# Retention attention and a top-2 mixture of experts in one kernel: k read as f32 on SyncE's queue, tails of q and k in 1-KB rows, states 64 columns wide, PSUM in pairs of banks, and a listed order in place of a planner

## The chip, the cores and the metric

The kernel runs on one core of a Trainium2 chip. Its time is the device time of one execution in microseconds (us). Three runs of the kernel before are known. Their median is 423.11 us, the lowest is 417.48 and the highest 436.01. The execution that the profiler recorded took 420.08 us.

A core has five engines with a queue of instructions each: TensorE (PE) multiplies matrices, VectorE (DVE), ScalarE (ACT) and GpSimd (POOL) work elementwise, and SyncE (SP) issues transfers (DMAs). Each queue is worked off in order: an instruction that waits holds everything behind it on its engine. Sixteen DMA engines move the data. A DMA that SyncE or ScalarE issues is shown as hardware_dynamic in the profile; GpSimd's are software_dynamic, and these alone change the type of the data on the way (f32 to bf16) or take row numbers from a table.

## The reference

```python
# q, k, v: (8 batches, 8 heads, 576 positions, 64)
scores = q @ k.T / 8
ret    = scores * where(i >= j, gamma[head] ** (i - j), 0)     # gamma[h] = 1 - 2**(-5-h)
x      = (ret @ v) as 4608 rows of 512                         # a row: one position, its 8 heads
noisy  = x @ w_gate + log1p(exp(x @ w_noise)) * noise          # 8 experts
top2   = the two largest of each row, softmax over the two as weights
out    = sum over the two: weight * (relu(x @ w1[e]) @ w2[e])  # w1: 512x1024, w2: 1024x512
```

## The kernel before

**Attention.** Work goes in 16 units. Unit u is one batch and four of its heads; four units make a pair of batches (bp 0 to 3). Only the first 512 positions of a sequence are in the units; the last 64 of each are the tail, one per pair of batches. For a unit `load` (L621) brings q, k and v, `cast` (L663) scales q and v by powers of gamma and makes them bf16, `tr` (L692) transposes k and q on TensorE, `scores` (L717) makes masked scores inside blocks of 128 positions, `states` (L751) sums k times v over blocks, and `out_` (L784) adds what the scores and the states of earlier blocks give. `tail` (L827) does the same for the last 64 positions.

How the data come: q as f32 in rows of 2 KB and v as f32 in rows of 512 bytes, both on SyncE. k comes on GpSimd (L647, `go = nc.gpsimd if n == "k"`), which turns it into bf16 on the way, so no engine casts it. The tails are three loads of two DMAs each per pair of batches (L658), all on SyncE and in rows of 256 bytes. Until the units are done, raw k lies in the buffer of expert 2's weights (class `kb`) and raw q in that of expert 1's (class `wq`), so these weights are loaded after the last unit's k and q (the argument `after` of `weights`). v lies in `big`.

A state is a 64x64 block per head, but lies in a tile of 128 columns for two heads with zeros beside it. So a state is taken out of PSUM in two halves of 64 partitions (L450 `tb<-ps`), and five tiles are set to zero first (L527). Scores and outputs leave PSUM one bank (128x512) at a time (L744, L450 `xT<-ps`).

**Routing.** When the four units and the tail of a pair of batches are done, `route` (L895) makes its logits, picks the two experts, finds each row's place in each expert's list, and writes the rows of x to the table `xd` in DRAM (L1072, on SyncE).

**Experts.** Each expert has a list of up to 1216 rows in blocks of 128. `fetch` (L1166) gathers a block from `xd` (L1179, on GpSimd) and transposes it, `up` and `wide` multiply by w1 (L1261, L1287), `relu` (L1270 on ScalarE, L1272 on VectorE) takes the result out, `second` and `halves` multiply by w2 (L1349, L1368), and `finish` (L1378) scales the rows and writes or adds them to the output (L1397 and L1399, then L1405 on GpSimd). The first blocks of experts 0 to 2 hold rows of early pairs of batches (`CLOSE`), so they can run while attention goes on: these are `up` and its `second`. The weights of experts 0 to 2 are loaded on GpSimd (L1112, L1116), the others on SyncE and cast by ScalarE or VectorE (`weights3`).

**Order.** Each call of `Plan.op` (L237) records an operation with its cost, its engine or a choice of two, and its priority. `Plan.run` (L274) goes through the recorded operations with a model of the engines and picks the one that can start first; the table `ORDER` shifts priorities by stage, and `BIAS` weighs VectorE against ScalarE where both may take it. `warm` (L454) fills expected gaps of TensorE in the first 170 us with matmuls whose result is not used (L458).

## Time and profile before

| | |
|---|---|
| runs | 423.11 us median of 3 (417.48 to 436.01) |
| profiled execution | 420.08 us, of which the span from first to last instruction is 418.5 us |
| PE busy | 378.8 us of the span (91%) |
| DVE, ACT, POOL busy | 166.6, 255.2, 302.1 us |
| mean clock granted to TensorE | 0.966 of full |
| DMA | 93.75 MB in 112584 packets, 65807 of them under 512 bytes |

The profile's page and the answers of the trace are read as follows. A row of a group of instructions has the line of the kernel, the engine, the operation, what it writes and reads (`half<-ps`: from PSUM into a tile of class half), the shapes, the count, then the busy time in us and the mean of one in ns, and then the engine's idle time just before them and what ended it. A row of a stretch (`A:B`) has its length, the busy time and count of PE, PE's weight loads (PEld), DVE, ACT and POOL, then the granted clock of TensorE, the mean busy share of the 16 DMA engines (over 1 where an engine has packets of two queues at once), and the GB/s moved, counted by the size written. A row of a source line has the shortest, middle and longest duration in ns and the first and last start in us.

### The profile page before, as it was taken

Reading aid. Unit: us, or ns where it says so; the run is one execution under the profiler, and the core shown is the slowest. Engines: PE = TensorE matmul, PEld = TensorE weight load, DVE = VectorE, ACT = ScalarE, POOL = GpSimd, SP = SyncE. Lnnn points to the kernel's source line nnn. Section 1 sums busy time; section 2 is a strip of 40 time slices with the busy share of each in tenths; the row PEclk is TensorE's granted clock in tenths of the full one; section 3 lists DMA queues with packets and bytes.
Section 4 is the critical chain, followed back from the end, with each engine's and each line's share of the span. In section 5 each row is a group of like instructions: output and inputs, shape, how many; then the busy total and the mean of one; then the engine's idle time right before and its main releaser. Section 6 shows DMA issues by size and latency. Waiting matters only on the chain. (4 is left out here: it accounts for less than half of the span.)

```text
span 418.5 us, 11275 instructions
## 1 busy us (share of the span) xinstructions
PE 378.8 (91%) x4415; PEld 235.4 (56%) x4415; DVE 166.6 (40%) x512; ACT 255.2 (61%) x432; POOL 302.1 (72%) x333
## 2 busy tenths in 40 slices
PE   5779786959989889999999999999999999999991
PEld 2457665837768667775566544544554554454461
DVE  5856578694979959220224322113112101100001
ACT  1437676746778765555567777756675676554550
POOL 8997766696399746776577767787786687753882
PEclk9999899697999969999999999999999999999997
DMA  9998999999995999579999999999999999991894
GB/s 219 266 235 189 259 228 186 296 260 257 256 231 107 257 237 254 151 177 238 243 342 383 270 259 279 239 278 223 289 236 232 183 268 182 214 152 25 130 127 105
DMA packets 112584, 93.75 MB, mean 224 GB/s; under 512 B 65807, under 2 KB 89872, under 8 KB 112530
## 3 DMA queue, kind: packets, MB, share of 16 engines
q0 software_dynamic: 34512, 40.31, 52.5%
q1 hardware_dynamic: 75330, 52.53, 49.5%
q8 instruction: 35, 0.57, 0.6%
q10 hardware_dynamic: 2688, 0.18, 0.5%
q14 instruction: 19, 0.16, 0.2%
HBM read 72.97 MB, written 26.36 MB: 237 GB/s over the span
## 5 line engine op out<-in xcount | busy, mean ns | idle before, releaser
L1349 PE MATMUL ps<-W,half 128*128 128x512 bf16 x568 | 185.1, 381 | 0.0
L1287 PE MATMUL ps<-big,W 128*128 128x512 bf16 (+4 forms) x640 | 180.6, 329 | 0.0
L1270 ACT ACTIVATE half<-ps 128x512 bf16<-128x512 f32 (+5 forms) x186 | 93.1, 506 | 77.0 <-PE ps L1287 64.0
L1179 POOL DMA_INDIRECT xg<-xd,xi x80 | 84.9, 1061 | 36.8 <-issue 15.0
L1405 POOL DMA_INDIRECT out_dram<-half,pl x59 | 79.8, 1352 | 28.4 <-ACT half L1270 13.9
L1287 PEld LDWEIGHTS <-W 128*128 128x128 bf16 x640 | 62.6, 98 | 48.7 <-issue 1.0
L1349 PEld LDWEIGHTS <-half 128*128 128x128 bf16 x568 | 55.2, 98 | 60.3 <-issue 0.6
L1212 DVE COPY pl<-xg 128x3 f32<-128x3 f32 (+1 forms) x65 | 13.4, 207 | 117.6 <-DMA xg<-xd,xi 117.5
L744 DVE TENSOR_TENSOR half<-ps,mask 128x512 bf16<-128x512 f32 x64 | 40.4, 683 | 16.0 <-PE ps L736 9.9
L450 ACT ACTIVATE half<-ps 128x1024 bf16<-128x1024 bf16 (+1 forms) x36 | 35.0, 992 | 14.5 <-PE ps L1201 6.0
L683 POOL TENSOR_TENSOR half<-big,tab 128x512 bf16<-128x512 f32 x30 | 31.9, 1080 | 7.2 <-DMA big<-in_v_dram 4.4
L450 ACT ACTIVATE W<-big 128x1024 bf16<-128x1024 f32 x34 | 35.5, 1051 | 0.0
L1261 PE MATMUL ps<-half,W 128*128 128x256 bf16 (+1 forms) x288 | 31.1, 263 | 0.1
L450 ACT ACTIVATE tb<-ps 64x512 bf16<-64x512 f32 x32 | 18.9, 592 | 18.3 <-PE ps L769 18.1
L1397 ACT ACTIVATE half<-ps,pl 128x512 f32<-128x512 f32 x42 | 28.7, 682 | 0.1
L1399 DVE TENSOR_SCALAR half<-ps,pl 64x256 f32<-64x256 f32 (+1 forms) x21 | 11.9, 570 | 39.3 <-PE ps L1368 21.3
L1405 POOL DMA_INDIRECT out_dram<-half,xg x15 | 15.4, 1026 | 16.7 <-ACT half L1397 11.5
L1261 PEld LDWEIGHTS <-W 128*128 128x128 bf16 x288 | 24.6, 101 | 4.7 <-issue 0.2
L676 POOL TENSOR_TENSOR half<-W,tabq 128x1024 bf16<-128x1024 f32 x11 | 20.9, 1903 | 5.4 <-DMA W<-in_q_dram 4.4
L450 ACT ACTIVATE xT<-ps 128x512 bf16<-128x512 f32 (+1 forms) x39 | 19.7, 555 | 6.2 <-PE ps L885 4.2
L458 PE MATMUL ps<-mask,ident__61 128*128 128x512 bf16 x67 | 18.3, 403 | 5.2 <-DVE wgn L592 5.2
L769 PE MATMUL ps<-half,W 64*64 64x64 bf16 (+2 forms) x512 | 18.8, 220 | 3.1 <-issue 2.4
(181 smaller groups left out, 425.1 us busy)
## 6 DMA issues: line engine op xcount, KB each, us to landing
big<-in_moe_w_dram SPq DMA_DIRECT2D x40, 512.0 KB
W<-in_q_dram SPq DMA_DIRECT2D x32, 256.0 KB
big<-in_v_dram SPq DMA_DIRECT2D x14, 512.0 KB
W<-in_moe_w_dram POOLq DMA_DIRECT2D x12, 512.0 KB, 13.0
xd<-xg SPq DMA_DIRECT2D x16, 264.0 KB
W<-in_k_dram POOLq DMA_DIRECT2D x14, 256.0 KB, 10.2
xg<-xd,xi POOLq DMA_INDIRECT x80, 7.2
big<-in_v_dram SPq DMA_DIRECT2D x4, 256.0 KB
```

Of the source, the lines that this page charges most:

```text
L450: self.nc.scalar.activation(out, in_, Act.Copy)
L676: self.eng(e).tensor_tensor(o, i, tabq.t[:, 2 * hq:2 * hq + 2].unsqueeze(3).to_broadcast([P, 2, 8, HD]), Alu.mult)
L683: self.eng(e).tensor_tensor(o, i, t, Alu.mult)
L744: nc.vector.tensor_tensor(S.t.bitcast(BF16).rearrange("p (h c x) -> p h c x", h=2, c=2)[:, h], p[h].t.rearrange("p (c x) -> p c x", c=2), ...
L769: nc.tensor.matmul(o[h * HD:(h + 1) * HD, hp, n, :], lhsT=self.keys(kn, hq, c, r, 2 * hp + h)[:k], rhs=vv[:k, r, c, y].unsqueeze(1).to_bro ...
L1179: ins = nc.gpsimd.indirect_dma_start(out=x.t[:n, :], out_offset=None, in_=self.xd[:rows, :], in_offset=IOff(ap=xi.t[:n, h:h + 1], axis=0), ...
L1261: nc.tensor.matmul(pv()[:, f2, :], lhsT=w.t[:, o:o + P], rhs=xv()[:, di, :n], start=(di == 0), stop=(di == KD - 1))
L1270: self.nc.scalar.activation(o, i, Act.Relu)
L1287: self.mm = nc.tensor.matmul(p.t[:, :n], lhsT=w.t[:, o:o + P], rhs=xv()[:, di, :n], start=(di == 0), stop=(di == KD - 1))
L1349: self.mm = self.nc.tensor.matmul(po.t, lhsT=hv[:, c:c + P], rhs=self.W[e].t[:, o:o + DM], start=(f == 0), stop=(f == KF - 1))
L1397: nc.scalar.activation(y.t[:n, c], x, Act.Copy, scale=g()[:n])
L1405: ins = nc.gpsimd.indirect_dma_start(out=self.out[:, :], out_offset=IOff(ap=ix()[:n], axis=0), in_=y.t[:n, :], in_offset=None, bounds_chec ...
```

## The change

- **Order.** `ORDER`, `BIAS` and the choice in `Plan.run` go. A list `PLAN` of all 1899 operations by number sets the order of recording, with `d`, `a` or `p` where an operation may go to VectorE, ScalarE or GpSimd. Slots of buffers are still chosen as the list is gone through.
- **k.** All 18 DMAs of k go on SyncE, as f32, and `cast` gets a step on ScalarE that makes k bf16 (2 halves for the first two units, one operation of 128x1024 for each other).
- **Places of raw data.** k and q of units 0 to 11 share a class `raw` in the buffers of experts 1 and 2; those of units 12 to 15 lie in `big` beside v.
- **Tails.** k and q of a tail come in rows of 1 KB: four positions of one head side by side. Each of the 16 former DMAs becomes two of 64 rows, and each of them reads 4 heads of 16 rows (`b::2`, `g`). The scale of a tail's q then depends on row and place (`tabt`, some 25 small operations ahead), its transposes are 32 of 64x64, and the copy after them puts the positions in order. v's tail is as before.
- **States.** A state tile has 64 columns per block, is taken out in one copy of 128x512, and isn't set to zero ahead; the product with it (`inter`) is made per head, 12 matmuls of 64x64 in place of 6 of 128x128, and before the scores instead of after.
- **Pairs of banks.** The two banks of scores are masked in one VectorE operation of 128x1024, and the two banks of a unit's output are copied in one. v is scaled in one operation of 128x1024 per unit (from unit 2 on) in place of two.
- **Small.** The loads of noise and gates go from ScalarE's queue to SyncE's. Some scale factors are folded into an Exp.

The listing of the orders gives these counts: ScalarE has 308 rows (429 before), VectorE 600 (464), GpSimd 317 (292), SyncE 193 (143). Of the `relu` copies 85 go to VectorE (10 before) and 111 to ScalarE (186). The matmuls of `up`, `wide`, `second`, `halves` and `column` are the same 1640; 61440 of their 638976 columns stand ahead of the last matmul of the last `route` before, and 60416 now. There are 40 unused matmuls for warming (67 before).

```diff
@@ Plan.run
-        while ready:
-            pick = None
-            for o in ready:
...
-                key = (round(t * 20), o.prio, o.i)
...
+        for x in PLAN:
+            o = self.ops[int(x.rstrip("dap"))]
+            e = {"d": "DVE", "a": "ACT", "p": "POOL"}.get(x[-1]) or list(o.eng)[0]
+            c, taken = o.eng[e], []
+            for b in o.allocs:
+                taken.append((slot(b, taken), b))
@@ Kernel.__init__
-        pl.cls("tb", mk("tb", 5, [P, 2, 4, P], BF16))
+        pl.cls("tb", mk("tb", 8, [P, 2, 4, HD], BF16))
...
-        pl.cls("kb", [(ws[2][:, i * F:(i + 1) * F], None) for i in range(8)])
-        pl.cls("wq", [(ws[1][:, 2 * i * F:2 * (i + 1) * F].bitcast(F32), None) for i in range(4)])
+        rw = [x[:, 4 * i * F:4 * (i + 1) * F].bitcast(F32).rearrange("p (c x) -> p c x", c=2) for x in ws[1:] for i in range(2)]
+        pl.cls("raw", [(x[:, i, :], x) for x in rw for i in range(2)])
@@ load
-            self.raw = {"k": [pl.buf("kb", "att") for c in range(2)], "v": [pl.buf("big", "att") for c in range(2)]}
+            self.raw = {"k": pl.buf("raw", "k", 2) if u < 12 else pl.buf("big", "k", 2), "v": pl.buf("big", "att", 2)}
...
-                go = nc.gpsimd if n == "k" else nc.sync
-                got.append(self.inp(lambda e, s=s, t=t, c=c, m=m, go=go: go.dma_start(
...
+                got.append(self.inp(lambda e, s=s, t=t, c=c, m=m: nc.sync.dma_start(
@@ load_tail
-                self.inp(lambda e, n=n, t=t, b=b: nc.sync.dma_start(
-                    out=t.t[b * HD:(b + 1) * HD].rearrange("p (h d) -> p h d", h=E),
-                    in_=self.src[n][2 * bp + b, :, 512:, :].rearrange("h s d -> s h d")),
...
+                    for c in range(2):
+                        nc.sync.dma_start(out=t.t[s, c * 256:(c + 1) * 256], in_=x[2 * bp + c, b::2, 512:, :].rearrange("h (g r) d -> h g (r d)", r=4))
@@ cast
+        def k(e, c):
+            o, i, _ = parts(rk, kn, c)
+            nc.scalar.activation(o, i, Act.Copy)
@@ scores
-            for h in range(2):
...
-                pl.op("DVE", 0.69, ev, r=[p[h], mask], w=[(S, h)], prio=u, at="scores2")
...
+            pl.op("DVE", 1.22, lambda e, p=p, S=S: nc.vector.tensor_tensor(
@@ states
-            for h in range(2):
-                s = slice(h * HD, (h + 1) * HD)
-                self.copy(e, T.t[s, :, :, s], o[s])
+            self.copy(e, T.t, p.t.rearrange("p (y n d) -> p y n d", y=2, n=4))
@@ out_
-        for e in range(2):
...
-            pl.op({"ACT": 0.6, "DVE": 0.69}, 0, ev, r=[p[e]], w=[(xT, (hq, b, e))], prio=u, at="out_3")
...
+        pl.op({"ACT": 1.03, "DVE": 1.22}, 0, ev, r=[p], w=[(xT, (hq, b, 0)), (xT, (hq, b, 1))], prio=u, at="out_3")
@@ record
-            raw = pl.fifo["kb" if e == 2 else "wq", "att"] if e else []
+            raw = pl.fifo["raw", "k"] + pl.fifo["raw", "q"] if e else []
```

Two places in the orders are shown. The first is SyncE's queue about the tail of the pair of batches 2 before; W is raw q here, big is v, half a tail, xd the table of rows.

```order
L647 DMA big_77<-in_v_dram 128x8x128 x2
L635 DMA W_123<-in_q_dram 64x2x512 x4
L647 DMA big_78<-in_v_dram 128x8x128 x2
L658 DMA half_87<-in_k_dram 64x8x64 x2
L658 DMA half_101<-in_q_dram 64x8x64
L1072 DMA xd<-xg_110 128x2x264
L658 DMA half_101<-in_q_dram 64x8x64
L1072 DMA xd<-xg_111 128x2x264
```

The same queue now, at the tail of the pair of batches 1, where W holds raw k and raw q.

```order
L514 DMA W_126<-in_k_dram 128x8x128 x2
L503 DMA W_126<-in_q_dram 64x2x512 x2
L968 DMA xd<-xg_114 128x2x264
L514 DMA big_81<-in_v_dram 128x8x128 x2
L531 DMA half_95<-in_k_dram 64x1x256 x4
L968 DMA xd<-xg_117 128x2x264
L531 DMA half_96<-in_q_dram 64x1x256 x4
L968 DMA xd<-xg_116 128x2x264
```

What moved: the units' k stands in SyncE's queue now between q and v, and a tail's k or q is four DMAs of 64 rows of 256 numbers in place of two of 512 rows of 64 numbers.

The second place is GpSimd's queue about the last units before: L647 is a DMA of k, L676 and L683 cast q and v, L841 a tail, L1179 gathers rows for an expert, L1112 and L1116 load weights into W_123 (expert 1).

```order
L647 DMA W_124<-in_k_dram 128x8x128
L841 TENSOR_TENSOR half_95<-half_97,tab 128x512
L1179 DMA xg_116<-xd,xi_207 128x264 x2
L683 TENSOR_TENSOR half_87<-big_78,tab 128x4x2x64 x2
L1179 DMA xg_117<-xd,xi_207 128x264 x2
L676 TENSOR_TENSOR half_96<-W_123,tabq 128x2x8x64
L683 TENSOR_TENSOR half_97<-big_79,tab 128x4x2x64 x2
L1405 DMA out_dram<-half_91,xg_115 4608x512
L676 TENSOR_TENSOR half_88<-W_123,tabq 128x2x8x64
L1112 DMA W_123<-in_moe_w_dram 128x2x1024 x2
L996 TENSOR_TENSOR ub<-MM,bnd 128x144
L683 TENSOR_TENSOR half_84<-big_79,tab 128x4x2x64 x2
```

The same queue now about the last units: L561 and L566 cast q and v, L720 and L723 are the tail, L1075 gathers, L1008 and L1012 load the weights of expert 1 into W_126.

```order
L561 TENSOR_TENSOR half_83<-big_79,tabq 128x2x8x64
L1075 DMA xg_119<-xd,xi_210 128x264 x2
L1075 DMA xg_120<-xd,xi_210 128x264 x2
L1075 DMA xg_121<-xd,xi_210 128x264
L566 TENSOR_TENSOR half_83<-big_80,tab 128x4x4x64
L1008 DMA W_126<-in_moe_w_dram 128x2x1024
L1075 DMA xg_121<-xd,xi_210 128x264
L561 TENSOR_TENSOR half_94<-big_81,tabq 128x2x8x64
L1008 DMA W_126<-in_moe_w_dram 128x2x1024
L566 TENSOR_TENSOR half_84<-big_80,tab 128x4x4x64
L1012 DMA W_126<-in_moe_w_dram 128x4x512
```

What moved: no k is issued here any more, the casts of q read `big` (units 12 to 15), a unit's v is one operation, and expert 1's weights are issued from before the cast of unit 14's q on, where they stood behind the cast of the last unit's q.

709 lines of the change are left out of this document (376 added, 333 removed), and 151 rows, old and new, of the table ORDER.

## The prediction

> **What bounds the kernel now.** I read the page's groups of instructions first, then the stretches of the span, then single source lines about the end of attention. In the stretches, the second column is PE's busy time.
>
> ```profile
> 0.00:160.00 160.00, 128.87 (x2835) 98.44 (x2836) 116.33 (x361) 100.19 (x162) 119.96 (x179) 0.93 1.11 232
> 160.00:410.00 250.00, 249.91 (x1582) 136.99 (x1580) 49.43 (x150) 155.04 (x271) 180.75 (x153) 1.00 1.01 223
> 410.00:419.00 9.00, 0.00 (x0) 0.00 (x0) 0.88 (x2) 0.00 (x0) 1.43 (x2) 0.73 0.28 89
> ```
>
> From 160 to 410 us PE is busy for 249.91 of 250 us at full clock; behind it stand 9 us of last rows. So the kernel has two parts. In the second one only PE counts:
>
> ```profile
> L1349 PE MATMUL ps<-W,half 128*128 128x512 bf16 x568 | 185.1, 381 | 0.0
> L1287 PE MATMUL ps<-big,W 128*128 128x512 bf16 (+4 forms) x640 | 180.6, 329 | 0.0
> L458 PE MATMUL ps<-mask,ident__61 128*128 128x512 bf16 x67 | 18.3, 403 | 5.2 <-DVE wgn L592 5.2
> ```
>
> Neither of the two products ever found PE idle (0.0 in the last column). Their count stays, and so does the share of them that stands ahead of the last routing. The change can therefore win or lose only what moves the start of that unbroken stretch. In the first 160 us PE is busy for 128.87 us, 18.3 of which are matmuls that warm (L458, all before 170 us), so 110.6 us of work stand in 160 us. No other engine is full there either: VectorE 116.33, ScalarE 100.19, GpSimd 119.96. What is full are the DMA engines:
>
> ```profile
> 0.00:126.00 126.00, 98.61 (x2271) 74.60 (x2275) 88.90 (x267) 75.21 (x119) 95.67 (x145) 0.93 1.16 240
> 126.00:129.00 3.00, 3.00 (x110) 2.59 (x104) 2.59 (x12) 2.00 (x3) 2.80 (x4) 1.00 0.09 24
> ...
> 15.00:18.00 3.00, 2.29 (x25) 1.37 (x26) 2.93 (x9) 2.19 (x3) 2.67 (x23) 1.00 1.20 283
> 27.00:30.00 3.00, 2.90 (x103) 2.35 (x105) 0.89 (x2) 1.78 (x3) 3.00 (x3) 1.00 1.45 194
> 60.00:66.00 6.00, 5.50 (x207) 4.81 (x197) 5.59 (x13) 3.78 (x6) 3.93 (x10) 1.00 0.59 120
> 102.00:105.00 3.00, 3.00 (x89) 2.38 (x88) 2.28 (x3) 2.33 (x6) 1.05 (x2) 1.00 1.07 335
> 138.00:141.00 3.00, 2.92 (x36) 2.34 (x33) 2.62 (x5) 2.46 (x6) 2.69 (x4) 1.00 1.08 337
> ```
>
> The last two columns are the DMA engines' share and GB/s. Loads fill them until 126 us (share 1.16) and then stop (0.09): the load stage ends there. Its mean is 240 GB/s, but it isn't even. At 102 and 138 us, where rows of x go to the table (1056 bytes each) with little beside them, 335 and 337 GB/s move. At 60 us it is 120 GB/s at a share of 0.59, and SyncE's queue says what ran:
>
> ```profile
> 50.90 7.42 SPq L658 DMA_DIRECT2D half<-in_k_dram  x2
> 58.43 3.64 SPq L658 DMA_DIRECT2D half<-in_q_dram  x2
> 62.17 2.10 SPq L658 DMA_DIRECT2D half<-in_v_dram  x2
> ```
>
> These are a tail's six loads, in rows of 256 bytes. They hold SyncE for 13.2 us, and nothing behind them gets out.
>
> Compute follows the loads late:
>
> ```profile
> L647 SPq DMA_DIRECT2D big<-in_v_dram x18: 373/657/5160, 1.0 to 108.5; - x18
> L647 POOL DMA_DIRECT2D W<-in_k_dram x18: 764/910/970, 1.7 to 113.3; - x18
> ...
> L683 POOL TENSOR_TENSOR half<-big,tab x30: 1037/1047/2017, 19.6 to 133.4; 128x512 bf16<-128x512 f32 x30
> ...
> L804 PE MATMUL ps<-half,half x512: 212/216/312, 28.1 to 137.0; 64*64 64x128 bf16 x171
> ```
>
> The last v is issued at 108.5 us, but its last cast on GpSimd starts at 133.4, and the last unit's output product at 137.0.
>
> **The change, part by part.** The sum is made against the profiled execution: 420.08 us, a span of 418.5 and 1.6 around it. It lies between the median of the runs (423.11) and their lowest (417.48), so I make no shift between the two.
>
> *Loads (k as f32, tails in 1-KB rows).* The page's list of DMAs gives the sizes.
>
> ```profile
> W<-in_k_dram POOLq DMA_DIRECT2D x14, 256.0 KB, 10.2
> W<-in_k_dram POOLq DMA_DIRECT2D x4, 128.0 KB, 6.4
> half<-in_v_dram SPq DMA_DIRECT2D x8, 128.0 KB
> ```
>
> k is 14 x 256 + 4 x 128 KB = 4.19 MB as bf16, so 8.39 MB as f32. The stage moves 240 GB/s x 126 us = 30.2 MB now and 34.4 MB after. No row shows k as f32 on SyncE, so I bound the stage by rates. If all went at the 337 GB/s of rows of 1 KB, it would take 102 us. If all went at the stage's own mean of 240, 143 us. I take it by kinds. k and v are both rows of 512 bytes: 16.8 MB at the 283 GB/s of the stretch at 15 us, where v is loaded, make 59.3 us. The tails of v stay at 256 bytes: 8 x 128 KB = 1.05 MB at 120 GB/s make 8.7 us. The remaining 16.6 MB at 337 make 49.2 us. With 1 us before the first load this is 118 us in place of 126: **-8 us**, the nearest rows for each kind. The ends are -23 and +17. That k beside other loads cost much already is seen at 27 us: k and a tail together filled the engines to 1.45, and 194 GB/s came out.
>
> *GpSimd.*
>
> ```profile
> L647 POOL DMA_DIRECT2D W<-in_k_dram x18 | 16.1, 895 | 0.3 <-issue 0.3
> L527 POOL MEMSET tb<- 128x1024 bf16 x5 | 4.7, 962 | 0.1
> L683 POOL TENSOR_TENSOR half<-big,tab 128x512 bf16<-128x512 f32 x30 | 31.9, 1080 | 7.2 <-DMA big<-in_v_dram 4.4 <-ACT xT L450 2.7
> L676 POOL TENSOR_TENSOR half<-W,tabq 128x1024 bf16<-128x1024 f32 x11 | 20.9, 1903 | 5.4 <-DMA W<-in_q_dram 4.4 <-DVE ps L943 0.9
> ```
>
> It loses 18 issues (16.1 us), five memsets (4.7), and pays 13 x 1903 + 2 x 1080 = 26.9 us for v in place of 31.9. Together that is 25.8 of 119.96 us. Most of it stands beside loads. On the path is only what lies between the last loads and the last cast, where the queue is late by some 20 us: between 0 and the 5.0 of the casts. I take **-3 us**.
>
> *ScalarE and VectorE in attention.*
>
> ```profile
> L450 ACT ACTIVATE tb<-ps 64x512 bf16<-64x512 f32 x32 | 18.9, 592 | 18.3 <-PE ps L769 18.1
> L450 ACT ACTIVATE xT<-ps 128x512 bf16<-128x512 f32 x31 | 17.1, 598 | 1.9 <-PE ps L814 1.9
> L450 ACT ACTIVATE W<-big 128x1024 bf16<-128x1024 f32 x34 | 35.5, 1051 | 0.0
> L837 ACT ACTIVATE half<-half 128x512 bf16<-128x512 f32 x4 | 2.5, 633 | 0.7 <-DMA half<-in_k_dram 0.7
> L744 DVE TENSOR_TENSOR half<-ps,mask 128x512 bf16<-128x512 f32 x64 | 40.4, 683 | 16.0 <-PE ps L736 9.9 <-ACT xT L450 5.9
> ```
>
> ScalarE gets k's casts, 14 x 1051 + 4 x 633 = 17.2 us. It gives up 18.9 - 16 x 0.598 = 9.3 us at the states and 17.1 - 14 x 1.051 = 2.4 at the outputs. Net +5.5 us, on an engine that is idle for 60 of the first 160. No row shows the masking of two banks at once: its bounds are 2 x 683 ns each, so nothing saved, and 683, which would save 21.9 us over 32. I take the first, since the work is per column. VectorE isn't on the path as long as the loads are: 0. k's cast is a new step between load and transpose, 1.05 us per unit, hidden while the loads are two units ahead; if they are not, each late unit pays it. On PE the transposes of k halve (128 matmuls gone). The noise and gate loads join SyncE's queue, eight issues among some 150. All 0.
>
> *Weights of experts 1 and 2.* k and q of the last four units lie in `big`, so these weights are waited for no longer by the last loads.
>
> ```profile
> 140.00:160.00 20.00, 16.93 (x202) 11.99 (x201) 14.71 (x50) 13.32 (x24) 11.29 (x17) 0.83 1.12 239
> ```
>
> PE idles for 3.1 us here, while their DMAs run. I take **-1 us** (0 to -3).
>
> *Experts.* 75 `relu` copies and some 25 others go to VectorE. At no more than 0.75 us each (the next row) they add 75 us at most to its 49.43 in 250 us. PE hides this, since no product found it idle. If that cover goes, each copy that comes late costs PE up to 0.75 us; at half load I expect none: 0.
>
> ```profile
> L1399 DVE TENSOR_SCALAR half<-ps,pl 128x512 f32<-128x512 f32 x7 | 5.2, 749 | 13.2 <-PE ps L1349 10.4 <-ACT half L1270 2.7
> ```
>
> The sum: -8 - 3 - 1 = -12 us, so 420.1 - 12 = **408 us**.
>
> **The rivals.**
>
> *The tails run on four engines.* A 1-KB tail load reads four heads of 16 rows, so its outer count is 4, where the loads of q, k and v before have 64 or 128. If a DMA is split among engines by that count, four of sixteen carry it. The tails of k and q are 16 x 128 KB = 2.10 MB, 6.2 us at 337 GB/s on sixteen engines and 24.9 on four: +18.7 us on the engines that every later load needs as well. All of it on the path would make 427 us. The other twelve go on with what is queued, and a load two units ahead can be late, so I take half: **417 us**. For it: the stretch at 60 us, where SyncE was held at a share of 0.59, shows that the form of a load can leave engines idle. Against it: no load with so small a count was seen. By the Trainium skill ("DMA: Bandwidth & Descriptors", section "Why a DMA increments its semaphore by 16 and not by 1"), a DMA goes on the largest number of engines up to 16 that divides the slowest dimension on both sides, which here would be 4. No run here shows it yet.
>
> *The stage was not the loads'.* If VectorE's and PE's own chains set the pace of the units (the last cast stood 25 us behind the last v's issue), the loads end earlier and nothing else does: -1 to -4 us, **418 us**. For it: VectorE is busy for 116 of 160 us, and the change adds some 25 small operations and six transposed copies to it. Against it: DMA engines at 1.16.
>
> *Bytes written are the limit (the slower side).* k as f32 writes 4.19 MB more. If the stage stays at 240 GB/s it ends at 143 us, 17 later; with the -4 of the other terms, 433 us. It is 2% slower (428.5) from a rate of 34.4 MB / 138.4 us = 249 GB/s down. For it: the mean of the stage. Against it: 283 to 337 GB/s in stretches without k on GpSimd.
>
> That the change doesn't do what it says is no rival: the listed orders show each part.
>
> **How the numbers follow.** 2% is about what a measurement of this kernel can tell from no change: 411.7 us and below is faster, 428.5 and above slower. The forecast (402 to 413) has 0.52, four engines (411 to 421) 0.24, the loads not the bound (415 to 420) 0.14, bytes written (421 to 434) 0.10. Faster: most of the first (0.49), a quarter of the second (0.06), none else: 0.55. Slower: most of the last: 0.08, and 0.01 from the second. Same: 0.36. The range is 400 to 421. It leaves out the last case and what of the first lies below 400, since VectorE's and PE's own work must still fit. The forecast's own range is 402 to 413.
>
> **What would show it.** Right, if the DMA engines fall idle near 118 us, the tails hold SyncE for some 5 us each, and PE's unbroken stretch starts about 12 us earlier with the same 250 us behind it. The four engines would show as stretches of low GB/s at the tails with SyncE held as before. If the loads end early but the last unit's output product stays near 137 us, the second rival holds. A wait of L1349's or L1287's successors after 160 us would break the term of the experts, and a load stage past 130 us the first term.

## The result, and the profile after

The changed kernel takes 537.24 us (median of four runs, 535.77 to 540.11) where the kernel before takes 420.3 beside it: 1.295 times as long, with an interval of 1.2835 to 1.3061. I had forecast 408, and 421 at most. The profiled execution took 536.99 us (span 535.4, granted clock 0.89 in the mean). Some executions of a kernel, the kernel before among them, run a few per cent longer than its others, so each ratio is taken over the undisturbed ones alone, while medians are over all.

First the changed kernel's groups of instructions, which answer to the rows of L1349 and L1287 before; the last column is the engine's idle time ahead of them and what ended most of it.

```profile
L1245 PE MATMUL ps<-W,half 128*128 128x512 bf16 x542 | 182.0, 385 | 34.4 <-DVE half L1295 10.2
L1183 PE MATMUL ps<-big,W 128*128 128x512 bf16 (+4 forms) x635 | 183.3, 330 | 18.5 <-ACT half L1166 8.3
L1075 POOL DMA_INDIRECT xg<-xd,xi x80 | 82.8, 1035 | 124.1 <-PE ps L1245 45.0
L1166 ACT ACTIVATE half<-ps 128x512 bf16<-128x512 f32 (+5 forms) x111 | 54.0, 504 | 155.0 <-PE ps L1245 46.2
L1168 DVE TENSOR_SCALAR half<-ps 128x512 bf16<-128x512 f32 (+5 forms) x85 | 46.6, 564 | 117.5 <-PE ps L1183 83.1
```

A matmul of the two products costs what it cost before (385 and 330 ns in the mean, against 381 and 329; a few of them are missing from the trace). But they found PE idle for 0.0 us before, and now for 34.4 and 18.5. The stretches of the span tell the rest (columns as in the prediction: length, PE, PE's weight loads, VectorE, ScalarE, GpSimd, clock, DMA share, GB/s):

```profile
0.00:160.00 160.00, 110.26 (x2282) 86.93 (x2284) 99.34 (x255) 76.93 (x101) 80.25 (x136) 0.77 0.83 216
160.00:410.00 250.00, 196.92 (x1612) 115.77 (x1629) 94.77 (x260) 85.10 (x144) 117.90 (x125) 0.92 0.70 176
410.00:535.00 125.00, 102.56 (x563) 51.02 (x572) 37.08 (x81) 36.90 (x62) 77.93 (x57) 0.98 0.85 155
...
240.00:260.00 20.00, 16.70 (x106) 9.45 (x106) 4.06 (x13) 4.62 (x8) 4.00 (x4) 1.00 0.09 24
```

From 160 to 410 us PE works 197 us of 250, where it worked 249.91. No engine is full and neither are the DMA engines (0.70 against 1.01). Between 240 and 260 us next to nothing is moved (24 GB/s). The first 160 us are slower as well: PE works 110.26 us there instead of 128.87, at a granted clock of 0.77 instead of 0.93. So the time must be in what the engines wait for. Who waits for whom, for GpSimd, PE, VectorE and ScalarE of the changed kernel (us in total, times, longest):

```profile
POOL xg L1075 <- PE ps L1245: 45.0, 8, 19.6
...
PE ps L1245 <- DVE half L1295: 10.2, 7, 5.6
PE ps L1183 <- ACT half L1166: 8.3, 14, 1.1
...
DVE half L1168 <- PE ps L1183: 83.1, 32, 8.6
...
ACT half L1293 <- PE ps L1245: 49.3, 14, 8.9
ACT half L1166 <- PE ps L1245: 46.2, 13, 6.5
```

PE waits for the engines that empty PSUM, these wait for PE, and GpSimd holds its gathers back until PE has done certain products. So PE and the engines that empty PSUM wait in a circle, and one place shows it. These are VectorE's and PE's instructions from 353 to 360 us in the changed kernel (start, length, and in brackets the idle time ahead and what ended it):

```profile
359.58 1.41 DVE L1295 TENSOR_SCALAR half<-ps,pl 128x512 f32<-128x512 f32 x2 [8.37 <-PE ps L1245]
...
353.43 0.38 PE L1245 MATMUL ps<-W,half 128*128 128x512 bf16 x1
...
359.16 0.38 PE L1245 MATMUL ps<-W,half 128*128 128x512 bf16 x1
360.38 0.24 PE L1183 MATMUL ps<-big,W 128*128 128x192 bf16 x1 [0.84 <-DVE half L1295]
```

In the built program, the bank that the first of VectorE's two operations empties was finished by the matmul that starts at 353.43 and ends at 353.81. VectorE was idle, and yet it starts 5.8 us later, when PE has also finished a product in the *other* bank of the same two-bank tile (359.54). PE in its turn waits for VectorE at 360.38.

Counted in the built programs, the waits between instructions that share a PSUM tile but no bank of it are these (the last three kernels are those of the runs below):

```
kernel                                          waits between different banks of one tile
before                                            0
changed kernel                                  350  (PE 133, VectorE 110, ScalarE 107)
kernel before, its 8 banks as 4 two-bank tiles  487
changed kernel, recorded in time order          400
changed kernel, 8 single-bank tiles               0
```

Put against the trace, those of the changed kernel that ended last stand behind some 57 us of idle time on PE, 93 on VectorE and 70 on ScalarE. This is an estimate, worked out by laying the built program's instructions against the trace, and the times overlap, so they aren't a sum of time lost.

### The profile page after: what moved, and what is told of

Read it like the earlier page. It is cut to its first block, busy times and chain, and to the rows that moved or that the text cites. A ratio compares the mean times of both kernels' runs of the same rounds, so it can differ in the third digit from the quotient of the medians.

```text
span 535.4 us, 11328 instructions
## 1 busy us (share of the span) xinstructions
PE 409.7 (77%) x4453; PEld 253.7 (47%) x4484; DVE 231.2 (43%) x594; ACT 198.9 (37%) x306; POOL 276.1 (52%) x316
## 5 line engine op out<-in xcount | busy, mean ns | idle before, releaser
L1245 PE MATMUL ps<-W,half 128*128 128x512 bf16 x542 | 182.0, 385 | 34.4 <-DVE half L1295 10.2
L1183 PE MATMUL ps<-big,W 128*128 128x512 bf16 (+4 forms) x635 | 183.3, 330 | 18.5 <-ACT half L1166 8.3
L1075 POOL DMA_INDIRECT xg<-xd,xi x80 | 82.8, 1035 | 124.1 <-PE ps L1245 45.0
L1166 ACT ACTIVATE half<-ps 128x512 bf16<-128x512 f32 (+5 forms) x111 | 54.0, 504 | 155.0 <-PE ps L1245 46.2
L1168 DVE TENSOR_SCALAR half<-ps 128x512 bf16<-128x512 f32 (+5 forms) x85 | 46.6, 564 | 117.5 <-PE ps L1183 83.1
L1295 DVE TENSOR_SCALAR half<-ps,pl 128x512 f32<-128x512 f32 (+1 forms) x32 | 21.6, 681 | 50.7 <-PE ps L1245 34.1
L620 DVE TENSOR_TENSOR half<-ps,mask 128x1024 bf16<-128x1024 f32 x32 | 38.7, 1219 | 9.7 <-PE ps L614 4.9
L1293 ACT ACTIVATE half<-ps,pl 128x512 f32<-128x512 f32 (+1 forms) x31 | 19.6, 644 | 43.0 <-PE ps L1245 24.3
L566 POOL TENSOR_TENSOR half<-big,tab 128x1024 bf16<-128x1024 f32 (+1 forms) x15 | 26.8, 1793 | 4.6 <-DMA big<-in_v_dram 2.6
L644 PE MATMUL ps<-half,half 64*64 64x64 bf16 (+2 forms) x512 | 20.2, 231 | 4.5 <-ACT half L297 2.1
L614 PE MATMUL ps<-half,half 64*64 64x128 bf16 x512 | 19.7, 264 | 5.1 <-DVE half L620 3.8
L297 ACT ACTIVATE xT<-ps 128x1024 bf16<-128x1024 f32 (+1 forms) x19 | 16.2, 859 | 18.0 <-PE ps L692 12.6
L644 PEld LDWEIGHTS <-half 128*64 128x64 bf16 (+1 forms) x512 | 18.0, 125 | 8.0 <-issue 4.3
```

Of the source, the lines that this page charges most:

```text
L297: self.nc.scalar.activation(out, in_, Act.Copy)
L566: self.eng(e).tensor_tensor(o, i, tab.t[:, hs, y].unsqueeze(3).to_broadcast([P, 4, y.stop - y.start, HD]), Alu.mult)
L620: pl.op("DVE", 1.22, lambda e, p=p, S=S: nc.vector.tensor_tensor(S.t.bitcast(BF16).rearrange("p (h x) -> p h x", h=4), p.t.rearrange("p h ...
L644: nc.tensor.matmul(o[h * HD:(h + 1) * HD, hp, n, :], lhsT=kk[:k, r, c, y], rhs=vv[:k, r, c, y].unsqueeze(1).to_broadcast([k, n.stop - n.st ...
L1075: ins = nc.gpsimd.indirect_dma_start(out=x.t[:n, :], out_offset=None, in_=self.xd[:rows, :], in_offset=IOff(ap=xi.t[:n, h:h + 1], axis=0), ...
L1166: self.nc.scalar.activation(o, i, Act.Relu)
```

## The experiments

**How to compare them.** Kernels timed together stood on one chip, with the kernel before beside them, and the chips are not alike. On four of them the kernel before took 414 to 436 us, on three others 432 to 460, some 4% more; the changed kernel's relatives took 6 to 13% more there. So ratios are compared only among chips of the first kind, and wherever two kernels are set against each other closely I say that they ran on the same one.

**One bank to a tile, first timing.** The changed kernel with eight tiles of one bank; scores' mask and the unit's output copy become two instructions, one for each bank.

```diff
-        pss = [self.ps.tile([P, 2, 512], F32, name=f"ps{i}") for i in range(4)]
+        pss = [self.ps.tile([P, 512], F32, name=f"ps{i}") for i in range(8)]
...
-            self.copy(eng, o, p.t.rearrange("p e (x q) -> p e x q", q=16))
+            for e in range(2):
+                self.copy(eng, o[:, e], p.t[e].rearrange("p (x q) -> p x q", q=16))
```

> The changed kernel with its eight PSUM banks as eight tiles instead of four tiles of two banks; the listed order, the engines and the slots stay. The operations that take a pair write and read the same two neighbouring banks, but the two evictions that spanned both (the masking of the scores on VectorE, 32 times, and the copy of a unit's output, 16 times) become two instructions of half the width each. Theory A (banks tied by their tile: an instruction on one bank waits for the last instruction on the other bank of the same tile; the built program of the changed kernel has 350 waits of that kind between TensorE, VectorE and ScalarE, the kernel before has none): the waits go, TensorE is without gaps from about 160 us on, 405 to 430 us. Theory B (the listed order itself locks the in-order engines to each other): the order is the same, so the gaps stay, 510 to 550 us. Theory C (clock: TensorE is slow in the first 260 us because too few filling matmuls keep it busy; 42 listed instead of 70): fillings are the same, so the first 200 us stay slow and only the expert phase gains, 480 to 500 us.

And the other way round, the kernel before with nothing changed but its eight banks, which become the halves of four tiles:

```diff
-        pl.cls("ps", [(self.ps.tile([P, 512], F32, name=f"ps{i}"), None) for i in range(8)], exp=4, xt=2, rt=2, tl=2, rw=2, att=7)
+        pss = [self.ps.tile([P, 2, 512], F32, name=f"ps{i}") for i in range(4)]
+        pl.cls("ps", [(x[:, i, :], None) for x in pss for i in range(2)], exp=4, xt=2, rt=2, tl=2, rw=2, att=7)
```

> The kernel before with one change: its eight PSUM banks are allocated as four tiles of two banks. Order, engines, instructions and banks are those of the kernel before; the built program gets 487 waits between instructions on different banks of one tile, where it had none. Theory A (banks tied by their tile): far slower, 480 to 560 us, with gaps of TensorE ahead of the expert matmuls that end with VectorE or ScalarE on PSUM. Theories B (listed order) and C (too few filling matmuls): nothing that they speak of changes, 415 to 425 us.

Measured: 492.67 us, 1.137 [1.125, 1.150], and 493.15 us, 1.136 [1.118, 1.155]. Both stood on a chip of the second kind (the kernel before: 432 to 453 us). So both were timed again.

> The changed kernel with single banks (list's recording order and ties kept), timed again. Its first timing, 1.137, stands on a chip on which the kernel before took 432 to 453 us, and on such a chip the version without late ties took 492 us where another chip gave 432 to 440. If the 1.137 was the chip's, this one now lies near the version without ties, 1.045 (435 to 445 us, on a chip where the kernel before takes 414 to 436); if the ties of the list's order cost what the first timing says, near 1.137 (470 us and more), with gathers that wait for matmuls of up to 18 us later.

> The kernel before with its eight banks taken from four tiles of two, timed again for the same reason (its first timing, 1.136, is of the same chip). If two-bank tiles alone make the waits between banks that cost, 1.08 to 1.14 (450 us and more); if the 1.136 was the chip's, within 2% of the kernel before.

On a chip of the first kind (before: 416 to 433) they take 462.86 us, 1.110 [1.104, 1.117], and 465.88 us, 1.119 [1.107, 1.131]. The direction stands, the sizes were partly the chip's. The first timing of the single banks lies in the range of the clock theory (480 to 500), the second in that of none: 405 to 430 was missed because a second fault remains, as the next runs show. The clock theory doesn't hold as the main cause: the runs below that mend both faults keep the same few warming matmuls and come to 437 us. Two-bank tiles alone, with the same instructions in the same order, cost the kernel *before* 12%, and single banks give the changed one back 74 us of 537. Here are the groups of the two products, first of the kernel before with two-bank tiles, then of the changed kernel with single banks, both from the second timing:

```profile
L1350 PE MATMUL ps<-W,half 128*128 128x512 bf16 x568 | 186.1, 380 | 9.6 <-ACT half L1271 6.4
L1288 PE MATMUL ps<-big,W 128*128 128x512 bf16 (+4 forms) x640 | 180.7, 328 | 2.4 <-ACT half L1398 2.4
```

```profile
L1246 PE MATMUL ps<-W,half 128*128 128x512 bf16 x568 | 189.8, 388 | 3.0 <-DVE half L1296 2.8
L1184 PE MATMUL ps<-big,W 128*128 128x512 bf16 (+4 forms) x640 | 185.3, 335 | 6.5 <-DMA big<-xg 6.5
L1076 POOL DMA_INDIRECT xg<-xd,xi x80 | 81.7, 1022 | 87.1 <-PE ps L1246 35.5
```

The first pair of rows is a kernel whose products found no idle PE at all until its banks were paired; they now wait 12 us, mostly for ScalarE. That is the smaller part of its some 49 us; the rest is lost ahead of the experts, as the table of late starts below shows. In the second fence PE waits for VectorE for 2.8 us where it was 10.2, and no longer for ScalarE. The largest wait left there is for data (`big<-xg`), and the row of gathers says why they come late: GpSimd waits 35.5 us for PE's products before it issues them.

**The order in which operations are recorded.** Before, the planner's loop hands over the operations in the order of their planned starts (15 of them come after one planned over 3 us later). The list of the changed kernel fixes the same for each engine, but operations are recorded in the list's order, and there 599 of 1899 come after one planned over 3 us later. That matters in two places: which of two instructions on one tile counts as the earlier one, and to which matmul a gather is tied (`self.mm`, the last one recorded). First the order of record alone, two-bank tiles kept; then the same with single banks:

```diff
         assert len(order) == len(self.ops)
+        order.sort(key=lambda x: x[1])
```

> The changed kernel, two-bank tiles as they are, but its operations are recorded in the order of their planned starts instead of the order of the list. On each engine the order stays as listed; only what the recording order decides between engines changes: which matmul a row gather of GpSimd is tied to (each gather of the expert stage waits for the last matmul recorded ahead of it, and the list records matmuls ahead of a gather that it plans up to 17.8 us later), and which of two instructions on the banks of one tile goes first (400 such waits instead of 350). Theory A (banks tied by their tile carry nearly all of what single banks left open too): no gain, ratio to the kernel before 1.25 to 1.33. Theory D (the gathers wait for matmuls that come too late): the delay of 34 to 59 us that the single-bank run built up between planned 170 and 240 us, and the jumps after it, come from there, so 15 to 35 us less than the changed kernel, ratio 1.20 to 1.26. Theory B (order on each engine): unchanged, 1.29.

> Both edits together: eight single-bank tiles (with the two split evictions), and recording in the order of planned starts. No wait between banks is left, and gathers are tied to matmuls planned no later than they are. Theories A and D together: what is left against the kernel before is the late tails of q (GpSimd waited 9.8, 7.4 and 3.8 us for them in the single-bank run) and slow clock ahead of 160 us, ratio 1.02 to 1.09, TensorE without gaps over 2 us after 170 us. Theory B (the order on each engine locks the engines): still above 1.11, with gaps of TensorE in the expert stage spread over many waits.

With them, on the same chip as both second timings, the changed kernel's operations on single banks ordered by the loop of the kernel before in place of the list:

```diff
+    BIAS = dict(DVE=1.5, ACT=0.5)
...
-        for x in PLAN:
-            o = self.ops[int(x.rstrip("dap"))]
+        while ready:
+            pick = None
```

> Eight single-bank tiles as above, all loads, widths and operations of the changed kernel, but the order is no list: the planner of the kernel before orders them by its own rule (earliest start, then priority) without any table of corrections for this program, and picks engines itself. Theory B (the list's order is the loss): the ratio falls well under that of the single-bank run with the list (1.137), to 1.00 to 1.08. Theories A and D (banks and late gathers): an untuned order is worth less than a tuned one whose two faults are mended, ratio 1.04 to 1.12, above that of the run with both mended.

Measured: sorted with two-bank tiles 477.82 us, 1.150 [1.139, 1.160], below all three expected ranges; sorted with single banks 445.88, 1.066 [1.039, 1.093]; the loop's own order with single banks 448.47, 1.081 [1.065, 1.097]. So sorting the record takes 59 us off the two-bank kernel, and pairing costs 8% of the kernel before even in time order. The loop's own order on single banks is no better than the list. This alone doesn't clear the list, for the loop runs here without its table of corrections and its own plan ends at 436.5 us, the list's at 404.4; that the list's order loses nothing after 160 us once both faults are gone is shown by the last row of the table of late starts. The groups, two-bank tiles first, then single banks, both sorted:

```profile
L1246 PE MATMUL ps<-W,half 128*128 128x512 bf16 x543 | 180.1, 379 | 18.8 <-ACT half L1294 4.6
L1184 PE MATMUL ps<-big,W 128*128 128x512 bf16 (+4 forms) x633 | 180.3, 328 | 6.2 <-DVE half L1296 3.3
```

```profile
L1247 PE MATMUL ps<-W,half 128*128 128x512 bf16 x543 | 179.6, 381 | 5.0 <-DVE half L1297 3.6
L1185 PE MATMUL ps<-big,W 128*128 128x512 bf16 (+4 forms) x633 | 180.2, 330 | 1.4 <-DMA big<-xg 0.6
```

**The ties of the gathers alone.** The list's order of record is kept, and gathers are no longer held for a matmul: with single banks, with two-bank tiles, and with single banks and a sorted record.

```diff
-                if pace:
+                if False:
                     self.tc.add_manual_dep(ins.ins, self.mm.ins.name, mybir.DependencyInfo(
```

> The single-bank run with the list's own recording order (ratio 1.137), and the ties of the gathers to matmuls left out: a gather of the last stage starts as soon as its row list and its buffer are there. Theory D (the ties to late matmuls are what the recording order cost): as good as recording in planned order, ratio 1.05 to 1.08, no wait of GpSimd for TensorE ahead of gathers over 3 us. Theory D' (something else that the recording order decides): stays 1.11 to 1.14. If gathers run too far ahead without ties and take the DMA engines from the weights, TensorE waits for weights instead.

> The changed kernel as it is, two-bank tiles and the list's recording order, with the ties of the gathers to matmuls left out and nothing else. It is the fourth corner of a square: tied banks and ties 1.295, single banks and ties 1.137, single banks and no ties 1.045. If the two causes add up (theories A and D), 1.18 to 1.22. If each only starts to matter where the other holds the engines up, 1.10 to 1.15. If the ties matter only with single banks, 1.27 to 1.30.

> Single banks, recorded in planned order, and no ties of the gathers. Theory D (the recording order cost through the ties alone): the same as single banks without ties in the list's order, 1.03 to 1.06. If the recording order matters in another way too, under 1.03.

Measured: 437.66 us, 1.045 [1.028, 1.062]; 526.05 us, 1.264 [1.253, 1.278]; 436.9 us, 1.054 [1.041, 1.066]. The second is near the range for ties that matter with single banks alone (1.27 to 1.30). The largest of GpSimd's waits with single banks and no ties (list's order) have no row for PE ahead of a gather any more, but the queue's own pace (`issue`) and one wait of 13.0 us for VectorE in the routing:

```profile
POOL xg L1076 <- issue: 24.5, 59, 7.0
POOL out_dram L1302 <- issue: 17.6, 58, 0.3
```

and PE is full again in the middle of the experts, here in that kernel and then in the kernel before:

```profile
240.00:280.00 40.00, 39.77 (x232) 20.43 (x236) 19.84 (x46) 18.60 (x31) 27.91 (x25) 1.00 0.98 291
```

```profile
240.00:280.00 40.00, 40.00 (x224) 19.95 (x223) 7.45 (x25) 29.55 (x46) 29.55 (x27) 1.00 1.08 273
```

All in one table (ratios to the kernel before):

```
                                    two-bank tiles    single banks
list's order of record, ties        1.295             1.110
list's order of record, no ties     1.264             1.045
record sorted, ties                 1.150             1.066
record sorted, no ties              not run           1.054
```

With single banks the order of record counts through the ties (1.110 with them, 1.045 without, on the same chip). Beyond them nothing is told apart: sorted, it is 1.066 and 1.054, whose intervals overlap each other's and that of 1.045. With two-bank tiles it counts for more than the ties: freeing the gathers gives 3 points there, sorting 14. Where the time is lost is seen in how late operations start, against the starts of each kernel's own plan (medians in us over PE, VectorE and ScalarE, worked out from the built programs and the traces; both plans end at 404.4):

```
planned start        40    80   120   160   200   240   280   340   390
before              4.8   7.6  11.2  12.3  12.4  11.7  11.9  11.2  11.2
changed kernel     11.9  31.4  50.8  77.4  94.9 101.3 109.1 120.8 125.5
before, pairs      10.5  26.2  36.5  44.2  47.2  49.0  50.4  52.5  55.2
single banks        7.1  15.7  27.4  29.2  43.9  44.6  44.6  48.8  48.9
pairs, sorted      11.5  23.6  34.5  45.5  49.6  53.5  56.8  62.6  65.7
single, no ties     6.9  15.9  22.9  25.5  25.3  25.2  25.2  25.2  25.1
```

Paired banks lose time from the first unit on and go on losing; late ties lose it at a few gathers (160 to 200 us: 14.7). Of the 114 us that the changed kernel is later than the one before at a planned 390, 65 are there at 160 already. Without either fault, nothing is lost after 160 us. What remains, some 13 us, is lost ahead of 160 and nearly all of it ahead of 120, in the load stage. PE's busy time goes the same way: 378.8 us before, 409.7 in the changed kernel, 378.1 with both faults mended.

**What remains: the tails of q and k.** The waits of PE in the first 180 us of the version with neither fault (single banks, sorted, no ties; L736 transposes a tail, L722 and L717 are the scaling of its q and the copy of its k):

```profile
PE ps L736 <- POOL half L722: 8.8, 2, 7.8
...
PE ps L736 <- ACT half L717: 2.9, 1, 2.9
```

Four versions of the tail loads were tried, and one of k. First, each DMA of 64 rows as four of 16, one to a head (single banks, sorted, with ties):

```diff
-                        nc.sync.dma_start(out=t.t[s, c * 256:(c + 1) * 256], in_=x[2 * bp + c, b::2, 512:, :].rearrange("h (g r) d -> h g (r d)", r=4))
+                        for h in range(4):
+                            nc.sync.dma_start(out=t.t[b * HD + 16 * h:b * HD + 16 * h + 16, c * 256:(c + 1) * 256],
+                                              in_=x[2 * bp + c, b + 2 * h, 512:, :].rearrange("(g r) d -> g (r d)", r=4))
```

> The run with both edits (single-bank tiles, recorded in planned order; ratio 1.066) and one more: each load of q's or k's tails, 64 rows of 1 KB whose outermost count is 4, becomes four loads of 16 rows whose outermost count is 16; the same rows go to the same places, and SyncE issues 96 loads more at about 0.55 us. In that run TensorE waits 9.7, 6.8 and 1.7 us ahead of the tails' transposes for k or q that landed 6 to 12 us after the last issue. Theory T (four rows deep means four DMA engines, as the Trainium skill says under why a DMA increments its semaphore by 16, and that makes the tails late): tails land 3 to 6 us after their last issue, the two long waits shrink by about 10 us together, ratio 1.03 to 1.05 unless SyncE's issues take it back. Theory Q (the tails are late because the weights and the gathers of GpSimd's queue hold the DMA engines, q0 share 0.46 to 0.95 there): landing stays 6 to 12 us, and the issues add to it, ratio 1.07 to 1.10.

473.56 us, 1.131 [1.116, 1.146], against 1.066 without, and above both expected ranges. The loads land within 1.6 us of their last issue, but the 96 more issues cost more than that. SyncE's queue and PE's wait in this version:

```profile
74.89 12.66 SPq L533 DMA_DIRECT2D half<-in_k_dram  x16
...
88.14 8.97 SPq L533 DMA_DIRECT2D half<-in_q_dram  x16
...
PE ps L738 <- POOL half L724: 30.3, 4, 9.7
```

In these rows 0.56 to 0.79 us go by for each issue, and everything behind them in the queue stands. The next three start from the version with neither fault (1.054). All tails on ScalarE's queue; k as bf16 on GpSimd's queue again; no tails of q and k but q's first one, so that this kernel leaves out part of the attention:

```diff
-                        nc.sync.dma_start(out=t.t[s, c * 256:(c + 1) * 256], in_=x[2 * bp + c, b::2, 512:, :].rearrange("h (g r) d -> h g (r d)", r=4))
+                        nc.scalar.dma_start(out=t.t[s, c * 256:(c + 1) * 256], in_=x[2 * bp + c, b::2, 512:, :].rearrange("h (g r) d -> h g (r d)", r=4))
```

> The run before this one (single banks, planned order, no ties), with the loads of the tails of q, k and v issued on ScalarE's queue instead of SyncE's; 24 us more of issues on ScalarE over the first 140 us. In the runs with single banks TensorE waits 9 to 18 us for the tails' transposes, behind GpSimd or ScalarE, which wait for q's or k's tail, landed 5 to 12 us after its last issue. Theory Q (the tails stand behind some 2 MB of other loads in SyncE's queue): on a queue of their own they land 2 to 5 us after their last issue, those waits shrink to under 5 us together, ratio 0.01 to 0.03 under the run before this one. Theory T (1-KB rows whose outermost count is 4 lie on four DMA engines): they land as late as before, no gain. Rival: the issues and their waits for buffers hold ScalarE up in its order, and the ratio rises.

```diff
+                go = nc.gpsimd if n == "k" else nc.sync
-                got.append(self.inp(lambda e, s=s, t=t, c=c, m=m: nc.sync.dma_start(
+                got.append(self.inp(lambda e, s=s, t=t, c=c, m=m, go=go, n=n: go.dma_start(
```

> Single banks, planned order, no ties (ratio 1.054), and k loaded as in the kernel before: by GpSimd's queue, which makes bf16 of it on the way, instead of f32 by SyncE; ScalarE copies it from there as it did. k's loads write half the bytes, SyncE issues 18 loads less, GpSimd 18 more. In the two runs without ties the loads of q, k and v end 11 to 12 us later than in the kernel before (last main load issued at 126 instead of 115 us) at a DMA share of 0.95 instead of 1.11, and the expert stage starts about 13 us later: that is all that is left of the loss. Theory K (k as f32 makes the load stage longer: 4.2 MB more are written, at 250 GB/s 17 us): the loads end 8 to 17 us earlier, ratio 1.01 to 1.03. Theory L (the loads stand in SyncE's order behind buffers and tails): they end as late, or later by what GpSimd's work delays k, ratio 1.05 to 1.09.

```diff
+                    if n != "v":
+                        if bp or n == "k":
+                            return
+                        t = self.raw0
```

> Single banks, planned order, no ties (ratio 1.054), and the tails of q and k left out of the loads: the rows of q's first tail stay in a tile of their own and serve as q's and k's tail of all four batch pairs, so part of the attention is computed from other rows (30 loads of 64 KB on SyncE fall away, 16 to 18 us of issues and 1.9 MB). Theory R (what is left of the loss are the tails of q and k: the waits for them, and their place in SyncE's order): TensorE's waits of 8.8 and 2.9 us ahead of the tails' transposes go, the loads end 8 to 12 us earlier, ratio 1.00 to 1.03. Theory L' (the order of loads and buffers is the rest, tails or not): 1.04 to 1.06.

Measured: 449.91 us, 1.083 [1.074, 1.093]; 461.12, 1.102 [1.094, 1.110]; 425.53, 1.018 [1.011, 1.026]. The first is what its rival expected, the second lies above both of its ranges. A queue of their own doesn't help the tails: q's is used 11.1 us after its last issue in the second pair of batches, so SyncE's backlog isn't what delays it. In this list's order k as bf16 on GpSimd's queue is worse than k as f32 on SyncE's. That isn't the price of f32 by itself. The list places k's issues for SyncE's queue, GpSimd comes to the first of them at 5.71 us instead of 2.48, ScalarE still copies k, and the GB/s below (187 against 255) count k's bf16 at half the size. And without the tails the kernel is 1.8% slower than the one before, under the 2% that such a timing can tell from no change, though the interval stays above 1. The first 126 us of the version with neither fault, of that with k as bf16, and of that without the tails:

```profile
0.00:126.00 126.00, 91.11 (x2116) 70.44 (x2116) 90.78 (x266) 70.30 (x102) 69.49 (x127) 0.89 0.95 255
```

```profile
0.00:126.00 126.00, 78.65 (x1684) 61.48 (x1685) 75.42 (x233) 55.11 (x81) 70.94 (x135) 0.82 0.91 187
```

```profile
0.00:126.00 126.00, 96.01 (x2338) 74.36 (x2338) 98.53 (x289) 77.64 (x116) 79.00 (x134) 0.95 0.98 260
```

The rival of the four engines says *why* the tails would be slow: their outermost count is 4. The last version reads the same bytes with an outermost count of 16:

```diff
-                        nc.sync.dma_start(out=t.t[s, c * 256:(c + 1) * 256], in_=x[2 * bp + c, b::2, 512:, :].rearrange("h (g r) d -> h g (r d)", r=4))
+                        nc.sync.dma_start(out=t.t[s, c * 256:(c + 1) * 256], in_=x[2 * bp + c, b::2, 512:, :].rearrange("h (g r) d -> g h (r d)", r=4))
```

> Single banks, planned order, no ties (ratio 1.054), and the same loads of q's and k's tails with the outermost count 16 instead of 4: the 64 rows of a load lie on the partitions the other way round (row group ahead of head), which the row factors and the copy behind the transposes take into account (that copy becomes four of a quarter each, 0.2 us more on ScalarE or VectorE, four times in all). Number of loads, bytes and row length stay. Without q's and k's tails the ratio was 1.018, so these loads cost about 0.036. Theory T (a load whose outermost count is 4 is carried by four of the sixteen DMA engines and lands late for it): the tails land 3 to 6 us after their last issue instead of 5 to 12, the wait of 7.8 us ahead of the tails' transposes shrinks to under 3 us, ratio 1.02 to 1.035. Theory Q (the DMA engines are full, whichever of them carry the tail): landing and ratio stay, 1.045 to 1.065.

The last issues of q's tail on SyncE and the operation on GpSimd that waits for it, in the second and third pair of batches, with count 4 and then with count 16. By the built program this operation waits for the four loads of q's tail and for no other load; in the first fence the view names loads that count on the same semaphores.

```profile
65.55 3.37 SPq L532 DMA_DIRECT2D half<-in_q_dram  x4
...
106.63 1.14 SPq L532 DMA_DIRECT2D half<-in_q_dram  x2
...
80.82 1.03 POOL L722 TENSOR_TENSOR half<-half,tabt 128x512 bf16<-128x512 f32 x1 [10.34 <-DMA half<-in_v_dram]
114.06 1.04 POOL L722 TENSOR_TENSOR half<-half,tabt 128x512 bf16<-128x512 f32 x1 [8.10 <-DMA big<-in_q_dram]
```

```profile
67.45 3.42 SPq L532 DMA_DIRECT2D half<-in_q_dram  x4
...
106.87 1.18 SPq L532 DMA_DIRECT2D half<-in_q_dram  x2
...
77.86 1.03 POOL L722 TENSOR_TENSOR half<-half,tabt 128x512 bf16<-128x512 f32 x1 [6.90 <-DMA half<-in_q_dram]
109.88 1.04 POOL L722 TENSOR_TENSOR half<-half,tabt 128x512 bf16<-128x512 f32 x1 [3.06 <-DMA half<-in_q_dram]
```

From the end of the last issue to the start of its use: 80.82 - 68.92 = 11.9 and 114.06 - 107.77 = 6.3 us with count 4, 77.86 - 70.87 = 7.0 and 109.88 - 108.05 = 1.8 with 16. The landing is 4 to 5 us shorter. Whether the kernel is, isn't settled. This first timing gave 438.26 us beside 430.65 and no ratio with an interval; three of its executions lie at 433.83 to 434.4, two of the kernel before at 423.53 and 426.94, that is 1.016 to 1.026. So both counts were timed on one chip, and count 16 once more:

> The version with single banks, its record sorted and the gathers not tied, with its q and k tail loads of outermost count 4, timed again beside the next kernel. It stood at 1.054 [1.041, 1.066] of the kernel before. If the tails' outermost count costs what the landings of the two profiles say (4 to 5 us for each q tail that is waited for), this one is 5 to 15 us slower than the next; if the gap between 1.054 and some 1.02 was a difference of chips, both come out within 3 us.

> The same with outermost count 16 (and four small copies in place of one after the tail's transposes), on the same chip. By the four-engines rival 425 to 432 us beside 434 to 440 of the kernel at count 4; if the count doesn't matter, the same time as that one, within 3 us.

> The version with single banks, sorted record and free gathers, its q and k tails loaded at outermost count 16, timed once more, for an interval on a chip on which the kernel before takes 414 to 436 us. By the four-engines rival 1.015 to 1.035 of the kernel before, where count 4 stood at 1.054 [1.041, 1.066]; if the earlier landing is worth nothing, 1.04 to 1.065. On a chip on which the kernel before takes 432 us and more, neither is told apart.

492.0 and 494.1 us (1.130 [1.116, 1.145] and 1.139 [1.127, 1.151]), and 494.1 beside 446.13 without a ratio. Both chips are of the second kind, where stalls of their own (last section) add 55 us to the very kernel that took 436.9. There the counts give the same time. The landing is shorter there too: q's tails are used 11.6 and 6.1 us after their last issue with count 4, 3.6 and 1.9 with 16, and PE's waits at the tails' transposes go from 12.7 us to 1.0 without any gain in time. On a chip of the first kind the two were never timed side by side, so the size of the form's share stays open, between 0 and the 3.6 points that all the q and k tails cost together (1.054 against 1.018). The kernel without these tails also has 30 issues fewer on SyncE's queue, and no run takes the two apart.

No version beat the kernel before.

## Why the prediction was wrong

- **The step that failed first** is that the change "can therefore win or lose only what moves the start of that unbroken stretch". The trace of before was read rightly: PE had no gap there. I took that for a property of the work and not of how its instructions wait for each other. The change broke the stretch itself, and 53 us of PE's idle time stand ahead of the two products alone. Its start moved as well, and not by the -12 us of the sum: by the table of late starts operations planned at 160 us come 65 us later than before.
- **The pairs of banks** had a price only as wider instructions ("I take the first", nothing saved; "All 0"). What was not priced is that a tile is the unit by which instructions are made to wait. The line that makes four tiles of eight isn't among those of the diff ahead of the prediction; it is the `-` line of the first experiment. The instruction widths were indeed worth little (a mask of two banks took 1219 ns, against 2 x 683). The waits of banks on their neighbours cost 74 us in the changed kernel (537.2 to 462.9, chips of one kind) and 12% in the kernel before, alone.
- **"That the change doesn't do what it says is no rival: the listed orders show each part"** was the second failure. The orders show each engine's row, and these were what the list says. They don't show in which order operations of *different* engines are recorded, and from that follow the gathers' ties. They cost 25 us once the banks are single (462.9 to 437.7 on one chip), and less (11 us) while the banks hide them.
- **Loads, -8.** In the changed kernel the last main load is issued at 146.4 us, against 114.7 before, and with both faults mended at 125.8, 11 later: wrong in sign. The mended stage moved 255 GB/s in its first 126 us, not the 34.4 MB / 118 us = 291 that the sum of kinds came to. Part of that are the tails of q and k, counted as rows of 1 KB like any other: without them the last main load is issued at 115.0, where it was before. But then too the DMA engines fall idle only at 120 us, after 267 GB/s. So the other kinds were priced too high as well: 283 and 337 are rates of stretches of 3 us, and the 283 isn't one of 512-byte rows alone, for SyncE issues four loads of q in rows of 2 KB at its start. How much is due to which kind stays open.
- **GpSimd, -3.** The work fell nearly as worked out: 278.3 us over the whole span in the version with neither fault, against 302.1, so 23.8 where 25.8 were counted. I see none of it on the path: what GpSimd's casts of v wait for in that version is the loads (12.5 us).
- **ScalarE, VectorE and the experts, 0.** Right where the other faults are gone: 39.77 of 40 us of PE, with VectorE at 19.84 where it had 7.45 in the same 40 us before. The cover that the prediction named does hold; it was gone in the changed kernel because of the banks and the late gathers, not because of the copies' length. The sign named for it, waits of the successors of L1349 and L1287, is what the first fence above shows; it has another cause than the term of the experts.
- **Rival: four engines (417).** By the Trainium skill ("DMA: Bandwidth & Descriptors", section "Why a DMA increments its semaphore by 16 and not by 1") a DMA goes on the largest number of engines up to 16 that divides the slowest dimension on both sides. The trace agrees in the landing: 4 to 5 us earlier at count 16. It doesn't tell how many engines carried a load. The tails cost some 15 us in all (1.054 against 1.018, of about 418), between the half that the rival took and its whole of +18.7; how much of that is the count's is open.
- **Rival: the stage was not the loads' (418).** Not borne out: in the mended version, taking the tails' loads away made the stage and the kernel shorter. In the changed kernel itself no run separates the two.
- **Rival: bytes written (433).** The mended versions do land at 437, but hardly for its reason: without the tails, with all of k as f32, the kernel is at 1.018. That k as bf16 writes less and is slower speaks against it too, but GpSimd's queue explains that as well.

## What to carry to other kernels

Before buffers are merged into larger tiles, ask what the tile is to the code that makes instructions wait: where it tracks tiles and not the parts used, two engines that alternated freely on two buffers will take turns on one, and a stretch without a gap can lose its fullness although no instruction got longer. A listed order per engine is not the whole order; whatever is tied to "the last one recorded" depends on the order across engines as well. And when one fault hides another (freeing the gathers gave 3 points with paired banks and 6.5 with single ones), mend the larger first, on one chip, before the smaller is priced.

## What the runs showed of the hardware

Chips differ, and by kernel. The version with single banks, a sorted record and free gathers takes 436.9 us on one chip and 492.0 on another, 13% more, where the kernel before takes about 4% more. On the second the engines stand still together. The rows are PE's, ScalarE's and VectorE's of the same version with count 16 there (492.35 us); `remote` and `issue` mean that no instruction in the profile ended the wait:

```profile
262.47 0.65 PE L1186 MATMUL ps<-big,W 128*128 128x384 bf16 x3
277.84 0.48 PE L1186 MATMUL ps<-big,W 128*128 128x384 bf16 x1 [7.04 <-DVE half L1171]
...
261.71 0.33 ACT L1169 ACTIVATE half<-ps 128x192 bf16<-128x192 f32 x1 [3.77 <-issue]
277.33 0.33 ACT L1169 ACTIVATE half<-ps 128x192 bf16<-128x192 f32 x1 [8.05 <-remote]
...
277.23 0.56 DVE L1171 TENSOR_SCALAR half<-ps 128x384 bf16<-128x384 f32 x1 [23.74 <-remote]
```

By the built program VectorE's operation at 277.23 waits for one of PE's products and one of ScalarE's copies, which are in the first and the third row and ended at 263.12 and 262.04. It starts 14 us later, and from 270.8 us on PE and ScalarE stand as well. GpSimd issues gathers and writes of rows until 274.8. From 200 to 300 us PE is busy for 71.98 us there and for 99.24 on the other chip. Three steps in how late VectorE's and ScalarE's operations start (13 us at a planned 165 to 180, 18 at 205 to 210, 9 at 260 to 270; medians as in the table above) make up 40 of the 61 us between the two profiles. Such a trace also holds fewer records of semaphores (171 against 369 for that of one of GpSimd's queues), so what ended a wait is told less surely. Why these chips do so is open, and so is whether the changed kernel itself would take longer on them.

A smaller load isn't issued much faster: on SyncE one load of a tail's 16 rows of 1 KB took 418 ns in the median, one of 64 rows 534 (q) and 570 (k). So splitting these loads is paid on the queue.
